# A recurrence and a highway layer on one core: loads of eight tokens per partition, and a new list of the order of work

## The chip, the cores and the metric

The kernel runs on one core of one Trainium2 chip. The metric is the device time of one execution, in microseconds (us); less is better. A profile is one such execution, recorded by the hardware profiler. Its span reaches from the first to the last recorded instruction; the execution's own time is a little longer.

## The reference, cut to what matters

```python
sig = 1.0 / (1.0 + np.exp(-f_logit))            # x, f_logit: (4, 6336, 256) fp32
f = lower_bound + (1.0 - lower_bound) * sig
i = 1.0 - f
for t in range(S):                              # S = 6336
    h = f[:, t] * h + i[:, t] * x[:, t]
    y[:, t] = h
x = y.reshape(25344, 256)
H = np.maximum(x @ w_h, 0.0)
T = 1.0 / (1.0 + np.exp(-(x @ w_t + b_t)))
out = T * H + (1.0 - T) * x
```

A linear recurrence runs along 6336 tokens for each of 4 batches and 256 channels. Two products with 256 x 256 weights follow for each token, and a gate that mixes the first with the recurrence's own output. 52.4 MB are read and 26.0 MB are written.

## The kernel before, in words

**Units, fronts and backs.** The tokens are cut into 24 units of 1024 neighbouring tokens of one batch, and one last unit with the 4 x 192 tokens that are left, on 96 partitions. The units go round the four batches, so that four recurrences run in turn. A unit lies in SBUF with tokens on 128 partitions and 8 tokens in each. Its recurrence is the "front", its layer the "back". The first three units and the last are cut further (`CUTS`): unit 0 into fronts of 2, 2 and 4 tokens per partition, units 1, 2 and the last into two fronts of 4. So there are 30 fronts: pieces 0 to 6 are small, pieces 7 to 27 are whole units (3 to 23), pieces 28 and 29 are the last unit's. There are 26 backs, 0 to 23 of a whole unit each.

**How the tokens lie** is set by `run(piece)` (L108 to L111). It says how many neighbouring tokens one partition holds in one run, so how long a contiguous stretch of memory a load brings to it: 4 tokens are 4 KB of fp32 in 256 channels. Where a whole unit of 8 has runs of 4, partition p holds tokens 4p to 4p+3 of the first 512 and the same of the second 512. Three places undo it, so that the recurrence sees the tokens in order:

- `load` (L102, its DMA on L106) brings `f_logit` (tile `lt`) and `x` (tile `xt`).
- `b_pe` (L209 to L217) transposes pairs of neighbouring tokens (two bf16 values seen as one fp32 word) on the tensor engine (PE) into PSUM tile `bT`, 128 columns at a time, and writes them at a stride of `run // 2` words: of two words where the run is 4.
- `decay_act` (L201 to L207) reads PSUM tile `uT`, which holds one token index after the other, with the tokens of a run innermost: at a step of 128 fp16 values.

**One front** takes these steps; the letters are those of the list that is told of below. L, X: loads. U: the gate `u`, a sigmoid on ScalarE (ACT, L154). P: the product `bv` of u and x for one pair of token indices, on GpSimd (POOL, L160); p is the same on VectorE (DVE, L166), taken for the two pieces in `EARLY`. A: transposes of u by PE (L198). F: the decay `f`, for each half of the channels, on ACT (L205). B: transposes of the pairs (L215). S: the scan along the tokens on DVE (L230), which gives tile `y`.

**One back** takes: Z, G: the two products with weights on PE (L245), tiles `zp` and `gp`; T: the sigmoid `t` on ACT (L251); D: `d`, on DVE (L256); E: `e`, d times t, on DVE (L166); H: the other part of e, on GpSimd (L160); O: matmuls that sum and transpose back (L296, L297); C: the copy of the result out of PSUM on ACT (L303), and V for a part of the last backs on DVE (L303); R: the store (L309). Of e, `shared(j)` columns are GpSimd's: 512 of 1024 in every whole back.

DVE's e and GpSimd's work share a port to SBUF, and the kernel has the next GpSimd product wait for a DVE product ahead of it in the list (`gpsimd_mul`, `port`).

**The order of the work** is a list written out, `PLAN`, of 1079 letters. Each letter issues the next instruction (or group) of its kind, and a digit behind A, B, Z, G and O names the PSUM slot. A and B share two slots, Z, G and O share three. Every engine runs its own in the order of the list, and SP's queue holds all loads and stores in that order; an instruction that waits holds back all behind it on its engine. SBUF tiles rotate: five each for `lt` and `xt`, two each for `bv`, `t`, `d` and `e`.

Of the kernel before, what the change touches and what calls it, by code (L numbers as in the profile page):

```python
# [19 lines left out]
def kernel(  # L20
# [19 lines left out]
    P = 128  # L40
    NH = D // P
    NB = 8
# [14 lines left out]
    units = [(P, NB, b, NB, s0) for s0 in range(0, S - rest, NB * P) for b in range(B)]  # L57
    units.append((rest // 2, NB, 0, 2, S - rest))
    fronts, backs = [], []
# [6 lines left out]

    LASTQ = 2

    EARLY = [(0, 0), (2, 0)]

# [29 lines left out]
    def load(i, name, src):  # L102
        u, j0, j1 = fronts[i]
        np_, j = units[u][0], run(fronts[i])
        t = fs[i][name] = new(name, [NB, D], FP32)
        pin(nc.sync.dma_start(t[:np_, :j1 - j0].rearrange("p (k j) d -> p k (j d)", j=j), tokens(src, u, j0, j1, j)))  # L106

    def run(piece):  # L108

        u, j0, j1 = piece  # L110
        return min(4, j1 - j0, units[u][3])  # L111

    def shape(piece):

        u, j0, j1 = piece
        return units[u][0], j1 - j0
# [34 lines left out]
    def gate(i):  # L151
        np_, nb = shape(fronts[i])
        u = fs[i]["u"] = new("u", [NB, D], FP16)
        pin(nc.scalar.activation(u[:np_, :nb], fs[i]["lt"][:np_, :nb], AF.Sigmoid, scale=-1.0))  # L154
# [13 lines left out]
    def product(i, k, mul):  # L168
        np_, _ = shape(fronts[i])
        if "bv" not in fs[i]:  # L170
            fs[i]["bv"] = new("bv", [NB // 2, D, 2], BF16)
        mul(inner(fs[i]["bv"][:np_, k:k + 1])[:, 0], fs[i]["u"][:np_, 2 * k:2 * k + 2],
            fs[i]["xt"][:np_, 2 * k:2 * k + 2])

    def width(piece):
        np_, nb = shape(piece)
        return np_ * nb
# [23 lines left out]
    def decay_act(i, h):  # L201

        np_, N, j = shape(fronts[i])[0], width(fronts[i]), run(fronts[i])
        f = fs[i]["f", h] = new("f", [NB * P], FP16)
        pin(nc.scalar.activation(f[:, :N].rearrange("p (k q j) -> p k q j", q=np_, j=j),  # L205
                                 fs[i]["uT", h].rearrange("p (k j q) -> p k q j", q=np_, j=j), AF.Identity,
                                 scale=ncc[:, h:h + 1], bias=1.0))  # L207

    def b_pe(i, m, slot):  # L209
        (np_, nb), r = shape(fronts[i]), run(fronts[i]) // 2  # L210
        for bT, h in filled(fronts[i], m, slot, fs[i], "bT", BF16):

            t = bT.bitcast(FP32).rearrange("p (k q j) -> p k j q", q=np_, j=r)
            for k in range(nb // 2):
                pin(nc.tensor.transpose(t[:, k // r, k % r],  # L215
                                        fs[i]["bv"][:np_, k, h * P:(h + 1) * P].rearrange("p d j -> p (d j)").bitcast(FP32),
                                        ident_f[:np_, :np_]))  # L217
# [41 lines left out]
    SHARE = 512  # L259

    def shared(j):

        return SHARE if width(backs[j]) == NB * P else 0

    def e_cols(j, a, e):
        if "e" not in bs[j]:
# [3 lines left out]
    def e_dve(j):  # L270
        vector_mul(*e_cols(j, 0, width(backs[j]) - shared(j)))

    def e_pool(j):
        gpsimd_mul(*e_cols(j, width(backs[j]) - shared(j), width(backs[j])))
# [37 lines left out]
    def each(pieces, count):  # L312
        return [(i, k) for i, piece in enumerate(pieces) for k in range(count(piece))]

    def halves_of(pieces):
        return each(pieces, lambda p: len(halves(p)))
# [11 lines left out]
        "U": (lambda i, _: gate(i), each(fronts, lambda p: 1)),  # L328
        "P": (lambda i, k: product(i, k, gpsimd_mul), [p for p in products if p not in EARLY]),
        "p": (lambda i, k: product(i, k, vector_mul), [p for p in products if p in EARLY]),  # L330
        "A": (decay_pe, halves_of(fronts)),
# [7 lines left out]
        "D": (d_dve, each(backs, lambda p: NH)),  # L339
        "E": (lambda j, _: e_dve(j), each(backs, lambda p: 1)),  # L340
        "H": (lambda j, _: e_pool(j), [(j, 0) for j in range(len(backs)) if shared(j)]),
        "O": (o_pe, groups),
        "C": (lambda j, q: o_copy(j, q, nc.scalar.copy, 0, group(j, q)[2]), [p for p in groups if group(*p)[2]]),
# [3 lines left out]
    }  # L347

    PLAN = (
        "LLXXLXQQUUA0pFFB1PSLXLXLXLSA0B1UFFpSSWWA0PFFUXLXLB1PSA0PSUFFUPPG0G1Z2B1DDSZ0STTA0B1PPHEFFUPSXXLA0SPF"  # L350
        "FUO1B0O2LLXXA1PSSPCCFFUPG0G1B0PPPDSSDZ2Z0A1A0TTFFEZ2B1Z0A0TTUFG1G2SDDB1HPPPPHPO0O1B0UCCSSZ2A1G0Z1B0E"
        "DTFTPPSPPPA1O2G0O1DHFUCCB1A0G0Z2Z1SFTTA1B0DEPSLLLXXRXRRLXRRRFUPG2O0B1O1A0DPPHCCG2FSDZ0Z1A1B0G2EPSTTF"
        "UPO0O1B1DPPHCCA0G2Z0SFDZ1A1B0EPSTFTUPG2O0A1B0O1DPPHCCG2Z0FSDA0B1Z1EPRRRRXLLSTFTPO2G0B0O1DPUCCESZ0G2A"
        "1Z1TFDB0A1G0PHPSDTFUO2B1O1CCPPPHSA0G0Z2Z1B1DFTEPSA0G0O2TPFDPPHB0O1G0A1UCCFSXLRXRRLRRRLLRXXDZ2Z1B0A1E"
        "PSTTFPO0G2B1A0O1DPPHCUCFSG0Z2Z1B1A0DEPSTTFPG0O2B0O1A1DPPHUCFCSG0Z2DA1B0Z1EPSG0PTFTDPPHB1O2O1G0A0UCCS"
        "Z2B1Z1FTDEPXRXRRRLRSTPA0O0G2O1B1DPPHFCCSA0G0Z2Z1B1DUFTEPSA0G0O2TPFCO1B0A1G2DPPHCSFUDZ0Z1A1B0G2EPSTTF"
        "PLLRRXLXRRXRRDPPHO0O1B0A1CCSFUG0Z2Z1A1B0DTTFEPSPG0O2O1B0A1DPPHCCFUSZ2G0A1B0Z1DEPSTTFPG0O2O1B0A1DPPHC"
        "CFUSG2Z0B1Z1A0RLRRRRXLRXXLLDEPSTFTPG2O0B0O1A1DPPHCUCFSG2Z0B0Z1A1DTTFEPSG2O0B0O1A1PDPPHCUCFSG2Z0B0Z1A"
        "1TFTDEPSPG2O0B1A0G1UCFDPPHSDO2Z0B1A0Z1TFTCPSPG0B0A1EZ1O2FTCUDSG0A1Z1B0RRRRRXRREDHFFO2G0B1TCPSRO1A0O2"
        "PCCFDSERG0G1RDSHZ2Z0B1DFTTSZ2G1O0HTTSDDCO2G1EERDO0CDO2CVRO1RCVZ0RCVTRTEO2O1CVRR"  # L360
    )
    assert all(PLAN.count(k) == len(places) for k, (_, places) in kinds.items())
    todo = {k: iter(places) for k, (_, places) in kinds.items()}
# [31 lines left out]
```

## Time and profile before

| | |
|---|---|
| time, median of 6 runs | 215.42 us (214.95 to 216.1) |
| the profiled execution: time, span | 215.08 us, 213.3 us |
| its granted tensor clock | 0.988 |
| busy: DVE, ACT | 196.0 us (92%), 194.6 us (91%) |
| busy: PE, weight loads | 188.9 us (89%), 132.5 us (62%) |
| busy: GpSimd | 164.9 us (77%) |
| moved by DMA | 78.68 MB, mean 369 GB/s, the load and store queue 92.4% of 16 engines |

Busy times are those of records. A record of ACT or DVE is longer than the step from one start to the next, because the next begins while the last results are still written: of two gates in the middle the record is 2.2 us and the step 1.8 us. Where "step" stands below, it is the distance between the starts of two instructions with no wait between them. The heading "idle before" in a group's row is the time for which the engine had no record, and what ended most of that time is named behind it.

### The profile page before, as it was taken

How to read it: one execution, taken by the hardware profiler on the slowest of the kernel's cores; microseconds unless marked ns; L12 is line 12 of the kernel's file. 1: busy time of each engine (PE TensorE's matmuls, PEld its weight loads, DVE VectorE, ACT ScalarE, POOL GpSimd, SP SyncE). 2: the span in 40 equal slices, each digit the busy share in tenths (PEclk: the TensorE clock that was granted, in tenths of full speed). 3: DMA queues.
4: the chain of work that ended last, by engine and by line, in shares of the span. 5: the costliest groups of instructions: out<-in, count | busy, mean ns of one | idle time of the engine just before them, and what ended most of it. 6: DMA issues, size and time to landing. Idle time of an engine off the chain costs nothing.

```text
span 213.3 us, 4602 instructions
## 1 busy us (share of the span) xinstructions
PE 188.9 (89%) x1800; PEld 132.5 (62%) x1800; DVE 196.0 (92%) x156; ACT 194.6 (91%) x194; POOL 164.9 (77%) x134
## 2 busy tenths in 40 slices
PE   0477798889999999999999999999999999999861
PEld 0244665666766665776575777577667667676651
DVE  1598698999999999999999999999999999999971
ACT  4559989999999999999999999999999999996851
POOL 4268987989789988978988897898898889646500
PEclk9999799999999999999999999999999999999998
DMA  3999999999999999999999999999999998547085
GB/s 98 403 418 422 423 416 420 422 416 416 423 416 422 416 417 420 417 420 416 422 420 417 419 416 421 420 407 419 417 409 366 369 286 330 174 184 288 7 349 195
DMA packets 22726, 78.68 MB, mean 369 GB/s; under 512 B 2353, under 2 KB 2865, under 8 KB 22705
## 3 DMA queue, kind: packets, MB, share of 16 engines
q1 hardware_dynamic: 22160, 78.39, 92.4%
q8 instruction: 14, 0.23, 0.4%
q10 hardware_dynamic: 544, 0.00, 0.1%
q14 instruction: 8, 0.06, 0.1%
HBM read 52.43 MB, written 25.95 MB: 368 GB/s over the span
## 4 chain that ended last, share of the span: by engine, by line
PE 46%; ACT 28%; DVE 14%; issue 5%; DMA 2%; POOL 2%; SPq 0%; ACTq 0%; DVEq 0%
PE gp L245 12%; ACT f L205 10%; PE zp L245 9%; ACT t L251 8%; DVE y L230 8%; PE op L296 7%; ACT u L154 7%; PE op L297 7%; PE bT L215 6%; PE uT L198 6%; DVE d L256 5%; ACT o L303 3%; DMA xt<-in_x_dram 2%; POOL e L160 1%; DVE e L166 1%
## 5 line engine op out<-in xcount | busy, mean ns | idle before, releaser
L160 POOL TENSOR_TENSOR bv<-u,xt 128x512 bf16<-128x512 f16 (+1 forms) x98 | 112.0, 1175 | 27.1 <-DVE e L166 8.5
L230 DVE TENSOR_TENSOR_SCAN y<-f,y,bT 128x1024 bf16<-128x1024 f16 (+3 forms) x56 | 106.8, 1920 | 0.7 <-ACT f L205 0.2
L205 ACT ACTIVATE f<-uT,ncc 128x1024 f16<-128x1024 f16 (+3 forms) x60 | 67.5, 1143 | 1.1 <-PE uT L198 1.1
L256 DVE SCALAR_TENSOR_TENSOR d<-y,ncc,gp 128x1024 bf16<-128x1024 bf16 (+1 forms) x52 | 62.6, 1211 | 1.2 <-PE gp L245 1.0
L251 ACT ACTIVATE t<-zp,bt 128x1024 bf16<-128x1024 f32 (+1 forms) x52 | 61.4, 1279 | 1.5 <-PE zp L245 1.0
L245 PEld LDWEIGHTS <-w_sb 128*128 128x128 f16 x400 | 37.9, 98 | 37.0 <-issue 5.7
L303 ACT COPY o<-op 128x1024 f32<-128x1024 f32 (+2 forms) x50 | 54.3, 1189 | 5.4 <-PE op L297 5.4
L154 ACT ACTIVATE u<-lt 128x2048 f16<-128x2048 f32 (+3 forms) x30 | 54.0, 1802 | 5.4 <-DMA lt<-in_f_logit_dram 5.2
L160 POOL TENSOR_TENSOR e<-d,t 128x1024 bf16<-128x1024 bf16 x24 | 51.6, 2151 | 8.7 <-DVE e L166 7.4
L297 PE MATMUL op<-ident_b,e 128*128 128x128 bf16 (+1 forms) x400 | 50.5, 222 | 2.8 <-DVE e L166 1.7
L245 PE MATMUL gp<-y,w_sb 128*128 128x512 bf16 (+1 forms) x200 | 51.4, 384 | 0.9 <-DVE d L256 0.8
L296 PE MATMUL op<-diag,y 128*128 128x128 f16 (+1 forms) x400 | 50.6, 221 | 0.8 <-ACT t L251 0.7
L245 PE MATMUL zp<-y,w_sb 128*128 128x512 bf16 (+1 forms) x200 | 49.5, 376 | 1.0 <-DVE y L230 0.8
L297 PEld LDWEIGHTS <-e 128*128 128x128 bf16 (+1 forms) x400 | 45.1, 115 | 7.0 <-DVE e L166 2.0
L296 PEld LDWEIGHTS <-y 128*128 128x128 bf16 (+1 forms) x400 | 45.2, 115 | 2.3
L215 PE MATMUL bT<-ident_f,bv 128*128 128x128 f32 (+1 forms) x200 | 32.3, 285 | 7.7 <-DVE y L230 2.1
L198 PE MATMUL uT<-ident_h,u 128*128 128x128 f16 (+1 forms) x400 | 31.7, 224 | 7.0 <-ACT u L154 5.5
L198 PEld LDWEIGHTS <-u 128*128 128x128 f16 (+1 forms) x400 | 26.9, 100 | 14.4 <-ACT u L154 5.8
L215 PEld LDWEIGHTS bT<-ident_f,bv 128*128 128x128 f32 (+1 forms) x200 | 23.0, 145 | 15.6 <-POOL bv L160 3.8
L166 DVE TENSOR_TENSOR e<-d,t 128x1024 bf16<-128x1024 bf16 (+1 forms) x26 | 18.4, 712 | 0.7 <-ACT t L251 0.5
L230 DVE TENSOR_TENSOR_SCAN y<-f,bT 128x512 bf16<-128x512 f16 (+2 forms) x8 | 10.5, 1343 | 3.2 <-PE bT L215 3.2
L303 DVE COPY o<-op 128x512 f32<-128x512 f32 (+1 forms) x4 | 2.8, 689 | 1.8 <-PE op L297 1.1
(20 smaller groups left out, 8.8 us busy)
## 6 DMA issues: line engine op xcount, KB each, us to landing
out_dram<-o SPq DMA_DIRECT2D x48, 512.0 KB, 13.6
lt<-in_f_logit_dram SPq DMA_DIRECT2D x21, 1024.0 KB, 14.9
xt<-in_x_dram SPq DMA_DIRECT2D x21, 1024.0 KB, 16.1
lt<-in_f_logit_dram SPq DMA_DIRECT2D x5, 512.0 KB, 7.8
xt<-in_x_dram SPq DMA_DIRECT2D x5, 512.0 KB, 8.6
xt<-in_x_dram SPq DMA_DIRECT2D x2, 384.0 KB, 10.2
lt<-in_f_logit_dram SPq DMA_DIRECT2D x2, 384.0 KB, 16.2
lt<-in_f_logit_dram SPq DMA_DIRECT2D x2, 256.0 KB, 4.1
```

Source lines behind the costliest of these rows:

```text
L154: pin(nc.scalar.activation(u[:np_, :nb], fs[i]["lt"][:np_, :nb], AF.Sigmoid, scale=-1.0))
L160: ins = pin(nc.gpsimd.tensor_mul(out_, a, b))
L198: pin(nc.tensor.transpose(uT[:, j * np_:(j + 1) * np_], fs[i]["u"][:np_, j, h * P:(h + 1) * P], ident_h[:np_, :np_]))
L205: pin(nc.scalar.activation(f[:, :N].rearrange("p (k q j) -> p k q j", q=np_, j=j), fs[i]["uT", h].rearrange("p (k j q) -> p k q j", q=np_, ...
L215: pin(nc.tensor.transpose(t[:, k // r, k % r], fs[i]["bv"][:np_, k, h * P:(h + 1) * P].rearrange("p d j -> p (d j)").bitcast(FP32), ident_ ...
L230: pin(nc.vector.tensor_tensor_scan(y, fs[i]["f", h][:, c:c + w], fs[i]["bT", h][:, c:c + w], 0.0 if prev is None else prev, op0=ALU.mult, ...
L245: pin(nc.tensor.matmul(p[:, a:e], w_sb[:, k, ki, h * P:(h + 1) * P], y_of(j)[:, ki, a:e], start=ki == 0, stop=ki == NH - 1))
L251: pin(nc.scalar.activation(bs[j]["t"][:, m, :width(backs[j])], bs[j]["zp", m], AF.Sigmoid, bias=bt[:, m:m + 1]))
L256: pin(nc.vector.scalar_tensor_tensor(bs[j]["d"][:, m, :width(backs[j])], y_of(j)[:, m], ncc[:, m:m + 1], bs[j]["gp", m], op0=ALU.mult, op1 ...
L296: pin(nc.tensor.matmul(o, y[:, h, cols], diag[:, h], start=True, stop=False))
L297: pin(nc.tensor.matmul(o, bs[j]["e"][:, h, cols], ident_b, start=False, stop=True))
L303: pin(copy(bs[j]["o", q][:np_, a:e], bs[j]["op", q][:np_, a:e]))
```

## The change

A run may hold eight tokens, so the 21 whole units that are one front (pieces 7 to 27) are loaded with 8 KB per partition in one stretch where there were two of 4 KB; the pairs of those pieces are written at a stride of four PSUM words instead of two, and their f is read with eight tokens innermost. Loads of pieces 0 to 6, 28 and 29, and all stores, keep their shapes. `EARLY` is empty: the first product of piece 0 and of piece 2 moves from DVE to GpSimd. The first three backs leave GpSimd no part of e: DVE makes all of it in one instruction of twice the size, and the list has three letters H fewer. The list is another one throughout; its first two and last two lines are shown.

```diff
-    EARLY = [(0, 0), (2, 0)]
+    EARLY = []
...
     def run(piece):
         u, j0, j1 = piece
-        return min(4, j1 - j0, units[u][3])
+        return min(8, j1 - j0, units[u][3])
...
     def shared(j):
-        return SHARE if width(backs[j]) == NB * P else 0
+        return SHARE if width(backs[j]) == NB * P and j >= 3 else 0
...
     PLAN = (
-        "LLXXLXQQUUA0pFFB1PSLXLXLXLSA0B1UFFpSSWWA0PFFUXLXLB1PSA0PSUFFUPPG0G1Z2B1DDSZ0STTA0B1PPHEFFUPSXXLA0SPF"
-        "FUO1B0O2LLXXA1PSSPCCFFUPG0G1B0PPPDSSDZ2Z0A1A0TTFFEZ2B1Z0A0TTUFG1G2SDDB1HPPPPHPO0O1B0UCCSSZ2A1G0Z1B0E"
...
-        "1TFTDEPSPG2O0B1A0G1UCFDPPHSDO2Z0B1A0Z1TFTCPSPG0B0A1EZ1O2FTCUDSG0A1Z1B0RRRRRXRREDHFFO2G0B1TCPSRO1A0O2"
-        "PCCFDSERG0G1RDSHZ2Z0B1DFTTSZ2G1O0HTTSDDCO2G1EERDO0CDO2CVRO1RCVZ0RCVTRTEO2O1CVRR"
+        "XLLLXXLXLQQUUA0A1PFFFUFUB0PSSB1A0FFPSSPB1A0XLLXLXXPFUFSSWWPB1A0G0Z1PFFUPSSDPXLLXLB0A1G2Z0PUTFFTPPB1S"
+        "SDUSSEZ1A0G0G2A1DDPFTFFPPZ1A0B1O0O2PSSTFECCUB0Z1B1G0G2SDSDA0Z0TUFTPPPPPPA0G1B1FXLLLXRRXLXDESA0Z0Z2O1"
...
+        "UCFPSO1PZ0CDTB1A0Z1G2SFTUHO0A0B1DFG1EPPPPSO2A0CCZ0DFB1O2Z1B0TCUTSESHPPG0A1Z2G1DDRRRRRRRRFFTA1B0O2Z0Z"
+        "1FCFSEHTTG2B1G0O1RSDDCO2SRHCZ0G1STRO2TDDEZ0CTERTG1O2O0DVDVCO2CREVO1CRO0RCVRR"
```

More of the change, by code (lines that the diff above doesn't have):

```diff
@@ L349 @@
     PLAN = (
-        "LLXXLXQQUUA0pFFB1PSLXLXLXLSA0B1UFFpSSWWA0PFFUXLXLB1PSA0PSUFFUPPG0G1Z2B1DDSZ0STTA0B1PPHEFFUPSXXLA0SPF"
-        "FUO1B0O2LLXXA1PSSPCCFFUPG0G1B0PPPDSSDZ2Z0A1A0TTFFEZ2B1Z0A0TTUFG1G2SDDB1HPPPPHPO0O1B0UCCSSZ2A1G0Z1B0E"
-        "DTFTPPSPPPA1O2G0O1DHFUCCB1A0G0Z2Z1SFTTA1B0DEPSLLLXXRXRRLXRRRFUPG2O0B1O1A0DPPHCCG2FSDZ0Z1A1B0G2EPSTTF"
-        "UPO0O1B1DPPHCCA0G2Z0SFDZ1A1B0EPSTFTUPG2O0A1B0O1DPPHCCG2Z0FSDA0B1Z1EPRRRRXLLSTFTPO2G0B0O1DPUCCESZ0G2A"
-        "1Z1TFDB0A1G0PHPSDTFUO2B1O1CCPPPHSA0G0Z2Z1B1DFTEPSA0G0O2TPFDPPHB0O1G0A1UCCFSXLRXRRLRRRLLRXXDZ2Z1B0A1E"
@@ L355 @@
[L355 to L358, printed above, removed]
-        "1TFTDEPSPG2O0B1A0G1UCFDPPHSDO2Z0B1A0Z1TFTCPSPG0B0A1EZ1O2FTCUDSG0A1Z1B0RRRRRXRREDHFFO2G0B1TCPSRO1A0O2"
@@ L360 @@
-        "PCCFDSERG0G1RDSHZ2Z0B1DFTTSZ2G1O0HTTSDDCO2G1EERDO0CDO2CVRO1RCVZ0RCVTRTEO2O1CVRR"
+        "XLLLXXLXLQQUUA0A1PFFFUFUB0PSSB1A0FFPSSPB1A0XLLXLXXPFUFSSWWPB1A0G0Z1PFFUPSSDPXLLXLB0A1G2Z0PUTFFTPPB1S"
+        "SDUSSEZ1A0G0G2A1DDPFTFFPPZ1A0B1O0O2PSSTFECCUB0Z1B1G0G2SDSDA0Z0TUFTPPPPPPA0G1B1FXLLLXRRXLXDESA0Z0Z2O1"
+        "UFTCTB0G0A1O1O2SDPPPFCCB1A0Z1G0O2FTUCB0G1PPPHPSDSEDPA1Z0Z2B0O1FTUCTESA1G0G1B0DDHPPPPSZ2O0O1FUTCCB1SA"
+        "0G2Z0B1FDUTPHPPSXXLRLRRRLRXLRRZ1A0G2O0PDTFCEEG1B1A0O2O0UFCCDSG1B0A1Z2Z0SDPHPPPPFTTA1B0O2O1G0HPSFCCZ2"
@@ new lines @@
+        "B1A0Z1DUTFTEG0O2PSPLXXRXRRRRDPPHCB1SA0O1G0Z2B1FCUTDEPSG1Z0A0O2FTCPDPPHB1A0Z1G0O2SFTCDEB0Z1A1G0PLLXRR"
+        "RRSDPPPUFTO2B0A1Z0G1SHDCFTEO2B0G0Z1A1PPPPCUFTSDHO2B0A1G0Z1SCFTO2B0A1DEPSZ1G0PPPCUFTDHO2B0A1O0G1SCFCD"
+        "EZ2B0A1Z0PSTFTPPPG1B1O2A0O0DUCFCSG1Z2A1B0HDELXLLRXRLLRXRRRRRXPSTFPPZ1G0O2B1DTCSZ1G2A0O0PHUFTCDEB1A0G"
+        "2Z1O0PSPFTCDPPHB0G1G2A1Z0UFTSA0B1FDEDSPO1O0Z2B0PPCCTPHSO1A1G0Z2B0UFTCDEPSA1G0Z2O1PPDB0FTCSA1Z2G0O1PH"
+        "FUCTDELXRRXXRRLRLXXRRRA1B0G0Z1PSFTO2DCB1A0G1Z0O2PPPHSUFCTDEB1A0Z1G2O0PSDFTCB0A1Z1G2SFPPPHDO0B1A0G2ET"
```

## The prediction

> **What bounds the kernel now.** I read the page's slices first (5.3 us each), then busy time by stretch, then ACT in the order of time at both ends.
>
> ```profile
> DVE  1598698999999999999999999999999999999971
> ACT  4559989999999999999999999999999999996851
> ...
> DMA  3999999999999999999999999999999998547085
> ```
>
> ```profile
> core 0: us, PE busy (x) PEld busy (x) DVE busy (x) ACT busy (x) POOL busy (x), PEclk, DMA share, GB/s
> 9.20:10.40 1.20, 0.58 (x2) 0.42 (x3) 0.88 (x2) 1.17 (x3) 0.00 (x0) 1.00 1.06 373
> 11.00:16.00 5.00, 3.79 (x21) 2.31 (x19) 4.74 (x6) 3.16 (x4) 3.12 (x3) 1.00 1.03 420
> 60.00:140.00 80.00, 77.23 (x769) 54.98 (x768) 79.53 (x55) 80.00 (x75) 70.12 (x53) 1.00 1.03 418
> ```
>
> Three things are full at once in the middle: DVE, ACT and the DMA engines. Which one sets the pace shows in the steps between starts. One unit costs ACT 1.80 (gate) + 2 x 1.00 (f) + 1.99 (two t) + 1.79 (two copies) = 7.58 us. DVE: 2 x 2.26 (scans) + 2 x 1.18 (d) + 0.58 (e) = 7.46. DMA: 3.15 MB at 418 GB/s = 7.53. PE: 16 product matmuls x 0.215, 32 of L296/L297 x 0.055, 16 transposes of u x 0.055, 8 of pairs x 0.109 = 6.95. The gates of pieces 11 and 26 start at 48.22 and 163.50: 7.69 us per unit. So ACT is the narrowest by a hair, and DMA's 7.53 lets loads run ahead: no gate waits for a load after 40 us. A faster DMA alone buys nothing there. What can be won lies at the ends, where ACT has gaps:
>
> ```profile
> 5.94 0.63 ACT L154 ACTIVATE u<-lt 128x512 f16<-128x512 f32 x1 [1.05 <-DMA lt<-in_f_logit_dram]
> ...
> 8.58 1.06 ACT L154 ACTIVATE u<-lt 128x1024 f16<-128x1024 f32 x1 [1.29 <-DMA lt<-in_f_logit_dram]
> ...
> 11.46 1.27 ACT L205 ACTIVATE f<-uT,ncc 128x512 f16<-128x512 f16 x2 [1.10 <-PE uT L198]
> ...
> 15.05 1.06 ACT L154 ACTIVATE u<-lt 128x1024 f16<-128x1024 f32 x1 [1.38 <-DMA lt<-in_f_logit_dram]
> ...
> 27.81 1.01 ACT L303 COPY o<-op 128x1024 f32<-128x1024 f32 x1 [0.89 <-PE op L297]
> ```
>
> ```profile
> 203.82 0.59 ACT L303 COPY o<-op 128x512 f32<-128x512 f32 x1 [1.14 <-PE op L297]
> ...
> 206.30 1.05 ACT L251 ACTIVATE t<-zp,bt 128x384 bf16<-128x384 f32 x2
> 208.63 0.58 ACT L303 COPY o<-op 96x512 f32<-96x512 f32 x1 [1.28 <-PE op L297]
> ```
>
> The brackets are ACT's idle time and who ended it. The first five (with two of 0.24 and 0.19) make 6.1 us; from 30.0 to 181 there is none. At the end ACT sits idle 1.14 us for a copy and only then does the last unit's t, on which e, the last matmuls and the last copies hang.
>
> **The parts, one by one.**
>
> *8 KB runs.* Between 9.2 and 10.4 us mostly the weights' 1 KB runs move, at 373 GB/s; 4 KB runs make 418 to 420. A fixed cost per run that explains both is 6 ns on each of 16 engines (43.9 ns per KB at 1 KB, 39.2 at 4 KB), and 8 KB would make 427 GB/s, my estimate from these rows: 2.46 us per 1 MB load for 2.51. The other end: 0. The 42 loads give 2.1 us of DMA time, nearly all hidden behind ACT's 7.58 us per unit; on the path lie the seven that come up to the load of lt of piece 10, 0.35 us. The Trainium skill speaks twice here: Perfetto Trace Analysis (DMA Optimizations) says that batching 2 KB into 4 or 8 KB can dramatically improve throughput, DMA: Bandwidth & Descriptors (Why small descriptors are slow) gives a few cycles per packet that matter at a few hundred bytes. The rows side with the second.
>
> *Pairs at a stride of four words.* The four transposes of one half, without waits: 0.60 us with a last record of 0.273, a step of 0.109 us for 128 columns, 0.85 ns a column, at a stride of two. The last unit's are at a stride of one: 0.083 us for 96, 0.86 ns. Contiguous is not faster, so I price four words at 0; it can't gain. The dear end is 0.213, this line's step at half clock (25.4 to 26.1 us): 8 x 0.104 = 0.83 us of PE per unit. PSUM — Partial Sum Buffer (Specifications, TRN2) has lines of 8 bytes and says that any non-contiguous pattern slows matmuls significantly, which speaks against this part; at a stride of two every word already has its own line, and the trace shows no cost. By that rule the sum would be that of the first rival.
>
> *f with eight tokens innermost.* Per added column, f costs 0.8 ns (0.41 us at 256 columns in runs of 2, 0.60 at 512 and 1.00 at 1024 in runs of 4), as the contiguous gate does (0.95 at 1024, 1.80 at 2048: 0.83). The step through PSUM stays 128 values. Price 0, since runs of 2 and of 4 lie on one line; dear end, the gate's rate, 0.03 ns x 1024 x 42 = 1.3 us; it can't gain, as 0.8 is there at either run.
>
> *No e on GpSimd for three backs, no product on DVE.* DVE: e of 2048 columns by the rows at 768 and 1024 (0.56 and 0.67) 1.1 us, 1.16 as two instructions, 0.58 before: +0.5 x 3; minus 2 x 0.62 for the products, of which the second is on the path. GpSimd: minus 3 x 2.13, plus 2 x 1.17. The matmuls that waited 1.11 us for GpSimd's e at 24.05 (and the copy behind them, 0.89) now wait for DVE. DVE's e holds GpSimd: the next product listed behind it waits. Behind e of back 0 that is P of piece 7, with 4 x 1.16 us up to its transposes: 27.4 to 32.1, needed at 33.2, so covered with 1 us left.
>
> *The new list, start.* Every load is as far back as the bytes ahead of it. The walk uses the trace's landings by place in the queue (4.24, 5.91, 6.73 us; then 0.63 per 256 KB). x now comes first, so the first gate starts at 5.94, not 4.26: 1.7 us later. Then, on ACT: gate, gate at 6.75, three f to 8.5, gate 2 to 9.45, f to 9.86, idle to 11.15 for lt of piece 3, gate 3 to 12.1, f of piece 2 to 13.3, idle 0.7 for transposes that wait for their PSUM slot, f 14.6, gate 4 to 15.55, f 16.15, idle 0.7, f of piece 4 to 18.05, gates 5 and 6 to 19.95, t, two f, t to 23.15, gate 7 to 24.95. Before, the same set ended at 25.89. Next f, t, f, f, t, f without a gap to 30.15 (DVE's second scan pair starts at 8.6 and its e of back 0 ends at 27.4, PE's O of back 0 after d of back 1, at 29.6), two copies to 31.95, gate 8 to 34.05 behind its load (32.25: one x load more is ahead of it than before, when it landed at 29.93). Before, this set ended at 35.82. Gates 9 and 10 end at 36.85 and 41.65; before, with one f moved to the same side, 43.43. **Gain at the start 1.8 us.** DVE is 2.4 ahead at that point (44.6 against 47.07 with the same set done), so it is not late next; the loads are, gate 10's by 0.3 us.
>
> *The new list, middle.* The same work per unit, in another order: price 0, ends -0.1 (what the old one loses: 7.69 - 7.58) and +0.25 per unit, half the 0.5 us that ACT waits at 200.74 for a copy. SP's queue has loads and stores mixed anew; the shortest leads of a load in the trace are 1.4 to 1.7 us (x of pieces 19 and 27, lt of 16).
>
> *The new list, end.* The last unit's Z and both t now stand ahead of the last whole back's copies: their 1.0 us fills ACT's idle 1.14 (and what copies 22 leave). DVE then has e right behind its own work. From the old last d's end (204.1), less the start's 1.8 (202.3): two of the copies' halves (0.6 each) now come ahead of e, and wait some 0.6 for ACT's halves, to 204.1, e to 204.6, two groups of O to 205.6, last copy 206.3, store 2.4 us to 208.7, where 212.2 was: 3.5 in all, **1.7 of it here**.
>
> **Sum.** The walks make 3.5 us. They charge nothing for hand-overs; ACT alone has idles of 0.16 to 0.68 us five times between 190 and 201 in the old list, which such a walk would miss. I keep three quarters: 2.6 us. Profiled execution: span 213.3 - 2.6 = 210.7, plus the 1.8 outside it, 212.5 for 215.08; the median of the six runs is 0.34 above that execution, so **212.8 us**.
>
> **Rivals.**
> 1. *The stride costs; slower.* Place: PE's transposes of pairs in pieces 7 to 27. PE has 7.58 - 6.95 = 0.63 us to spare per unit, so it decides from a step of 0.19. At 0.213 PE needs 7.78: +0.2 over 7.58 for 21 units, 4.2, and the waits of DVE's scans that PE with no slack brings, by 0.1 each unit 2.1. Less the gain of 2.6: 219. For it speaks only that the trace has no stride of four; against it, 0.85 and 0.86 ns.
> 2. *The new middle stalls; slower.* f, t and copies alternate singly where they ran in pairs, so every ACT instruction has another engine's hand-over ahead of it. At +0.25 per unit over 19 units: +4.7 - 2.6, 217.5. It decides from 0.14. Against it: PE has slack, and each engine's sum is unchanged.
> 3. *What is won at the start is lost to the loads or at the end.* Loads land 0.3 us ahead of gates 9 and 10, with no lead behind them; a hold of 1 us on each of two eats the start's gain, and the tail's order may hold at V, which waits for the ACT copy of the same group. 215.4.
> 4. *Runs of 8 KB are moved as 4 KB.* The start loses its 0.35: within the forecast's own range, 213.1.
>
> **Chances.** Forecast and rival 4, 211.3 to 214.7: 0.6. Rival 3, 214.8 to 216.0: 0.15. Rival 2: 0.15, half of it below 217.3. Rival 1: 0.1. The range 211.3 to 217.3 leaves out some 0.2. About 0.3% (0.65 us) is what this measurement can tell from no change: faster 0.6, within 0.15, slower 0.25.
>
> **What would show it.** Steps of L215 at 0.109 for 128 columns (rival 1: above). f at a step of 1.00. Gate 7 at 23 us and gate 8 near 32, with ACT's gap ahead of the copies at 27 us gone. The middle's GB/s up by some per cent while loads run ahead, or unchanged because ACT holds the buffers; 7.6 to 7.7 us between gates (rival 2: 7.9). No t among ACT's last four rows. I am wrong if gates late in the middle wait for loads, or if DVE's e of backs 0 to 2 takes over 1.6 us beside GpSimd's products.

## The result, and the profile after

| | before | after |
|---|---|---|
| time, median | 215.21 us (70 runs, 214.53 to 216.29) | 214.28 us (35 runs, 213.29 to 215.16) |
| ratio, 95% interval | | 0.9949 (0.994 to 0.9958) |
| the profiled execution: time, span | 215.08, 213.3 us | 214.35, 212.6 us |
| load and store queue, share of 16 engines | 92.4% | 90.4% |
| packets | 22726 | 17350 |

The kernel became 0.5% faster: 1.1 us by the ratio (0.9 by the medians) where 2.6 were forecast. First the page's slices of after (5.3 us each).

```profile
DVE  1269999999999999999999999999999999999980
ACT  2757999999999999999999999999999999997760
...
DMA  5999999999999999999999999999999996242465
```

DVE is now full from the fourth slice on and ACT from the fifth; before, it was the eighth and the seventh: the holes around 27 us are gone. But DVE's second and third slices are emptier (2 and 6 for 5 and 9). The same windows as before (the columns are those that the prediction shows):

```profile
9.20:10.40 1.20, 0.39 (x2) 0.00 (x0) 0.70 (x2) 1.20 (x3) 0.95 (x1) 1.00 1.02 416
11.00:16.00 5.00, 3.31 (x22) 2.49 (x20) 3.22 (x4) 3.05 (x5) 4.30 (x4) 1.00 1.04 410
60.00:140.00 80.00, 77.72 (x768) 54.79 (x766) 79.40 (x54) 80.00 (x75) 71.34 (x56) 1.00 1.02 423
```

The middle moves 423 GB/s for 418, within the estimate of 427, and ACT stays at 80.00 of 80: no stall, and no gain there either. From 11 to 16 us DVE works 3.22 us of 5 (4.74 before) and ACT 3.05 (3.16 before). ACT's rows there, in order of time:

```profile
5.91 0.63 ACT L154 ACTIVATE u<-lt 128x512 f16<-128x512 f32 x1 [3.11 <-DMA lt<-in_f_logit_dram]
7.47 0.63 ACT L154 ACTIVATE u<-lt 128x512 f16<-128x512 f32 x1 [0.93 <-DMA lt<-in_f_logit_dram]
...
11.85 1.06 ACT L154 ACTIVATE u<-lt 128x1024 f16<-128x1024 f32 x1 [1.27 <-DMA lt<-in_f_logit_dram]
...
15.17 0.69 ACT L205 ACTIVATE f<-uT,ncc 128x512 f16<-128x512 f16 x1 [1.10 <-PE uT L198]
...
18.73 1.27 ACT L205 ACTIVATE f<-uT,ncc 128x512 f16<-128x512 f16 x2 [1.36 <-PE uT L198]
...
24.93 1.93 ACT L154 ACTIVATE u<-lt 128x2048 f16<-128x2048 f32 x1
...
33.66 2.00 ACT L154 ACTIVATE u<-lt 128x2048 f16<-128x2048 f32 x1
```

Against the walk: gate 1 starts at 7.47 (6.75), gate 3 at 11.85 (11.15), f of piece 4 at 18.73 after 1.36 us of idle (0.7), gate 7 at 24.93 (23.15), gate 8 at 33.66 (32.25). So ACT ends gate 7's set 0.84 us later than before, where the walk had it 0.94 earlier. DVE in the same stretch:

```profile
14.16 2.45 DVE L230 TENSOR_TENSOR_SCAN y<-f,y,bT 128x512 bf16<-128x512 f16 x2 [1.32 <-PE bT L215]
16.53 2.30 DVE L148 SCALAR_TENSOR_TENSOR w_sb<-o,cc 128x512 f16<-128x512 f32 x2
18.75 2.32 DVE L230 TENSOR_TENSOR_SCAN y<-f,bT 128x512 bf16<-128x512 f16 x2
20.99 1.25 DVE L256 SCALAR_TENSOR_TENSOR d<-y,ncc,gp 128x1024 bf16<-128x1024 bf16 x1
22.16 2.44 DVE L230 TENSOR_TENSOR_SCAN y<-f,y,bT 128x512 bf16<-128x512 f16 x2
```

From 14.16 us (piece 2's scans) to its last d at 203.6 DVE's idle time sums to 0.9 us, none of it over 0.11 at once before 76 us (before: 4.5 us, from 13.31): DVE starts late and then hardly rests. The two W take 2.30 us together (1.39 before), because a product of GpSimd runs beside the second, from 17.09 on:

```profile
17.09 2.76 POOL L160 TENSOR_TENSOR bv<-u,xt 128x512 bf16<-128x512 f16 x2 [1.58 <-DMA xt<-in_x_dram]
```

The end, on ACT:

```profile
201.90 1.05 ACT L251 ACTIVATE t<-zp,bt 128x384 bf16<-128x384 f32 x2 [0.33 <-DVE e L166]
203.70 0.59 ACT L303 COPY o<-op 128x512 f32<-128x512 f32 x1 [0.75 <-DVE o L303]
204.82 0.59 ACT L303 COPY o<-op 128x512 f32<-128x512 f32 x1 [0.54 <-DVE o L303]
206.15 1.07 ACT L303 COPY o<-op 96x512 f32<-96x512 f32 x2 [0.74 <-DVE o L303]
```

As forecast no t is among ACT's last four instructions (all copies), and the last copy ends at 207.2 (209.8 before, there on DVE): 2.6 us won. But the last store, issued at 207.7, lands at 211.04, where before's landed at 212.20. The stores of either kernel's last 2 us, before first:

```profile
L309 SPq DMA_DIRECT2D out_dram<-o x2: 324/336/347, 209.2 to 209.8; - x2
...
DMA to landing us min/median/max: 2.4/2.4/2.4
```

```profile
L309 SPq DMA_DIRECT2D out_dram<-o x3: 333/377/572, 206.8 to 207.7; - x3
...
DMA to landing us min/median/max: 3.3/3.3/3.3
```

Of the 2.6 us won at the copy 1.2 arrive at the last landing, and 0.7 at the end of the span (1.53 us lie between them, 1.07 before).

### The profile page after: what moved, and what is told of

Same layout as the page of the kernel before. It is cut to its first block, busy times and chain, and to the rows that moved or that the text cites. A ratio compares the mean times of both kernels' runs of the same rounds, so it can differ in the third digit from the quotient of the medians.

```text
span 212.6 us, 4616 instructions
## 1 busy us (share of the span) xinstructions
PE 187.8 (88%) x1800; PEld 131.4 (62%) x1800; DVE 195.3 (92%) x154; ACT 193.7 (91%) x194; POOL 160.9 (76%) x133
## 2 busy tenths in 40 slices
DMA packets 17350, 78.69 MB, mean 370 GB/s; under 512 B 2352, under 2 KB 2864, under 8 KB 11952
## 3 DMA queue, kind: packets, MB, share of 16 engines
q1 hardware_dynamic: 16784, 78.39, 90.4%
## 4 chain that ended last, share of the span: by engine, by line
ACT 35%; PE 31%; issue 13%; DVE 13%; DMA 3%; SPq 1%; POOL 1%; ACTq 1%; DVEq 0%; POOLq 0%
ACT t L251 11%; PE zp L245 9%; ACT o L303 8%; ACT u L154 8%; ACT f L205 8%; PE gp L245 6%; DVE y L230 6%; DVE d L256 5%; PE bT L215 4%; PE uT L198 4%; PE op L296 3%; PE op L297 3%; DMA xt<-in_x_dram 3%; DVE e L166 1%; SPq L106 1%
## 5 line engine op out<-in xcount | busy, mean ns | idle before, releaser
L160 POOL TENSOR_TENSOR bv<-u,xt 128x512 bf16<-128x512 f16 (+1 forms) x100 | 114.6, 1181 | 31.6 <-DVE e L166 14.1
L205 ACT ACTIVATE f<-uT,ncc 128x1024 f16<-128x1024 f16 (+3 forms) x60 | 64.9, 1094 | 2.5 <-PE uT L198 2.5
L251 ACT ACTIVATE t<-zp,bt 128x1024 bf16<-128x1024 f32 (+1 forms) x52 | 62.8, 1226 | 0.4 <-DVE e L166 0.3
L154 ACT ACTIVATE u<-lt 128x2048 f16<-128x2048 f32 (+3 forms) x30 | 52.6, 1758 | 5.3 <-DMA lt<-in_f_logit_dram 5.3
L245 PE MATMUL zp<-y,w_sb 128*128 128x512 bf16 (+1 forms) x200 | 50.5, 377 | 0.9 <-DVE d L256 0.6
L296 PE MATMUL op<-diag,y 128*128 128x128 f16 (+1 forms) x400 | 49.2, 219 | 1.8 <-DVE d L256 0.7
L160 POOL TENSOR_TENSOR e<-d,t 128x1024 bf16<-128x1024 bf16 x21 | 44.8, 2135 | 7.3 <-DVE e L166 2.6
L297 PE MATMUL op<-ident_b,e 128*128 128x128 bf16 (+1 forms) x400 | 49.3, 219 | 0.0
L198 PE MATMUL uT<-ident_h,u 128*128 128x128 f16 (+1 forms) x400 | 32.1, 225 | 10.0 <-ACT u L154 7.5
L166 DVE TENSOR_TENSOR e<-d,t 128x1024 bf16<-128x1024 bf16 (+2 forms) x26 | 19.0, 736 | 0.1
L230 DVE TENSOR_TENSOR_SCAN y<-f,bT 128x512 bf16<-128x512 f16 (+2 forms) x8 | 10.4, 1336 | 4.1 <-PE bT L215 4.1
(19 smaller groups left out, 10.9 us busy)
```

The costliest lines, as they stand in the source:

```text
L160: ins = pin(nc.gpsimd.tensor_mul(out_, a, b))
L198: pin(nc.tensor.transpose(uT[:, j * np_:(j + 1) * np_], fs[i]["u"][:np_, j, h * P:(h + 1) * P], ident_h[:np_, :np_]))
L230: pin(nc.vector.tensor_tensor_scan(y, fs[i]["f", h][:, c:c + w], fs[i]["bT", h][:, c:c + w], 0.0 if prev is None else prev, op0=ALU.mult, ...
L245: pin(nc.tensor.matmul(p[:, a:e], w_sb[:, k, ki, h * P:(h + 1) * P], y_of(j)[:, ki, a:e], start=ki == 0, stop=ki == NH - 1))
L251: pin(nc.scalar.activation(bs[j]["t"][:, m, :width(backs[j])], bs[j]["zp", m], AF.Sigmoid, bias=bt[:, m:m + 1]))
L296: pin(nc.tensor.matmul(o, y[:, h, cols], diag[:, h], start=True, stop=False))
```

## The experiments

"ratio" is the time against the kernel before, with its 95% interval. Own times are those of profiled executions.

### The parts of the change, each alone

**Runs of eight in the old list.**

```diff
-        return min(4, j1 - j0, units[u][3])
+        return min(8, j1 - j0, units[u][3])
```

> The kernel before with runs of eight tokens and nothing else changed (its own list, its own e and products). My theory: ACT and DVE set the pace from 40 us on and hold the buffers, so faster loads buy only the start: the DMA rate in the middle rises from 418 to 422-424 GB/s, the pair transposes stay at a step of 0.109 us, and the time is 0 to 0.4 us below before (ratio 0.998 to 1.000). Rival: the whole gain of the change (1 us) is that of the runs; then this kernel stands at a ratio of 0.995.

215.20 us, ratio 0.9983 (0.9962 to 1.0004). Nothing that can be told from no change: the middle of the interval is a gain of 0.4 us, its end 0.8, and a cost of the stride of four words doesn't show.

**Runs of four in the new list** (the same line, the other way).

> The changed kernel with runs of at most four tokens again (new list, no e on GpSimd for three backs, no products on DVE). My theory: the list and not the runs made the gain, so 213.8 to 214.7 us, a ratio of 0.994 to 0.998. Rival: the runs made it; then a ratio of 1.000, or above if the list costs.

214.52 us, ratio 0.9955 (0.9938 to 0.9972). The gain is there without the runs; 0.24 us of median is what they add, not to be told from nothing.

**No e on GpSimd, no product on DVE, in the old list:** `EARLY = []`, `and j >= 3` in `shared`, the first three H left out, p written as P.

> The kernel before, its list kept, but GpSimd makes no part of e for the first three backs and all products of the first pieces (three letters H dropped, two p made P). My theory: DVE gains 1.2 us of products and pays some 1.6 us for e, and PE waits for the whole e instead of GpSimd's half; within 0.5 us of before (ratio 0.998 to 1.002). Rival: DVE's longer e is what held the start of the changed kernel: 1 us or more above before (1.005).

215.32 us, ratio 0.9988 (0.9963 to 1.0012). No difference.

### The end

**The old list with the new order at its end.** The first try took the new letters from the last unit's T on:

```diff
-...DFTTSZ2G1O0HTTSDDCO2G1EERDO0CDO2CVRO1RCVZ0RCVTRTEO2O1CVRR
+...DFTTSZ2G1O0HCSTRO2TDDEZ0CTERTG1O2O0DVDVCO2CREVO1CRO0RCVRR
```

> The kernel before, with the new list's order for the last instructions only, from the last unit's first t on. My theory: the last copy ends 1.5 to 2 us earlier, but the stores behind it find the DMA engines still busy with those issued just ahead, so the last store lands only 0.5 to 1.0 us earlier: ratio 0.995 to 0.998. Rival, the prediction's own: a store takes 2.4 us from its issue whatever is ahead of it, and all of 1.7 us is won: ratio 0.992.

218.57 us, ratio 1.0135 (1.0096 to 1.0174): a miss. Z of back 24 stayed in PSUM slot 2, as in the old list, and the new order's next O asks for that slot, so it waits until t has read it. ACT's rows:

```profile
200.45 1.01 ACT L303 COPY o<-op 128x1024 f32<-128x1024 f32 x1 [1.72 <-PE op L297]
...
204.01 1.01 ACT L303 COPY o<-op 128x1024 f32<-128x1024 f32 x1 [1.59 <-PE op L297]
```

Two waits of 1.7 and 1.6 us come from one digit. It says nothing of the order. The second try takes the slots along, from Z of back 24 on:

```diff
+...DFTTSO2HCZ0G1STRO2TDDEZ0CTERTG1O2O0DVDVCO2CREVO1CRO0RCVRR
```

> The kernel before, with the new list's order and PSUM slots for the last 41 instructions, from the two Z and G of the last unit's first back on, so that no slot of the old order is left to wait for. My theory: the last copy ends 1.5 to 2.5 us earlier than before (209.8), but the last three stores then stand behind 1.5 MB of other stores, and the end comes only 0.5 to 1.2 us earlier: ratio 0.994 to 0.998. Rival: a store always takes 2.4 us; ratio 0.990 to 0.992. Rival: the end of the list gained nothing and all of the 1 us is from elsewhere: 1.000.

214.97 us, ratio 0.9983 (0.9966 to 1.0). The last copy ends at 208.5 (209.8), the last store goes from 209.03 to 212.37, 3.3 us, where before's took 2.4: what the copies win, the store gives back. The start of this execution was slower: its last scan ends at 201.47 us (200.99). Counted from there, the last copy comes 1.7 us earlier than before (7.06 for 8.77), the last landing 0.3 (10.91 for 11.20).

**Which bytes make the last store long?** After with three quarters of back 23's stores left out:

```diff
+        np_ = units[u][0] // (4 if j == 23 else 1)
```

> The changed kernel, but of the last whole back's two stores only the first quarter of the partitions is stored (0.79 MB of output left out). My theory: at the end the DMA engines are the bound (the last copy ends at 207.2 and stores land until 211.0), so 0.79 MB at 420 GB/s less makes the last store land 2.4 to 2.8 us after its issue, 0.6 to 1.0 us earlier: ratio to before 0.990 to 0.992. Rival: the 3.3 us from issue to landing are the store's own; then no change from the changed kernel, ratio 0.995.

214.29 us, ratio 0.9941 (0.9917 to 0.9964), the same as after; the last store still takes 3.1 us. My theory named the wrong bytes. So the last unit's own, with five sixths of back 24's store left out:

```diff
+        np_ = 16 if j == 24 else units[u][0]
```

> The changed kernel, but the store of the last unit's first back goes out for 16 of its 96 partitions (0.33 MB of output left out). My theory: the last three stores, 0.79 MB in runs of 2 KB issued within 1 us, are what keeps the last one 3.3 us on its way instead of 2.4; with the first of them nearly gone the last lands 2.4 to 2.7 us after its issue: 0.6 to 0.9 us less than the changed kernel, ratio to before 0.991. Rival: 3.3 us whatever is ahead: 0.995.

213.22 us, ratio 0.9919 (0.9892 to 0.9947). The three last stores:

```profile
L310 SPq DMA_DIRECT2D out_dram<-o x3: 332/347/380, 207.5 to 208.4; - x3
...
DMA to landing us min/median/max: 2.0/2.2/2.5
```

The last takes 2.5 us where it took 3.3, and lands 10.0 us behind the end of the last scan instead of 10.9. So the bytes of back 24's store make this 0.9 us: in after the last unit's three stores (0.79 MB) are issued within 1 us and land 0.5 us behind one another; in the same last stretch before had two.

**Copies that don't share a group.** In backs 23 and 24, ACT's half of each group waits for DVE's (0.75, 0.54 and 0.74 us above). Here each group is copied whole, by one engine (the letters of the copies that this saves leave the list):

```diff
-        return q * size, g, g // 2 if size == QB else (g if q % 2 == 0 else 0)
+        return q * size, g, g if q % 2 == 0 else 0
```

> The changed kernel, but each of the last backs' groups is copied by one engine whole (even groups ACT, odd ones DVE) where ACT and DVE each took half of it; in the changed kernel's trace the two halves run one after the other (202.97, 203.70, 204.10, 204.82). My theory: the two groups of back 23 are copied side by side, their stores start up to 1 us earlier and the DMA engines, which hold the end, finish 0.5 to 1.0 us earlier: ratio to before 0.990 to 0.993. Rival: the last copy (205.4 to 207.2) holds the end, and it isn't touched: ratio 0.995.

214.19 us, ratio 0.9939 (0.9916 to 0.9963): not to be told from after. With the last e ahead of DVE's copy as well:

```diff
-...O2O0DVDVCO2CREVO1CRO0RCVRR
+...O2O0DDECVRO1O2RCRO0CVRR
```

> The changed kernel with whole copies (each group by one engine, as in the run with whole copies) and the last e put ahead of the copies of back 23 on DVE, the last matmuls behind it spread over the free slots. My theory: the last copy ends 0.6 to 1.0 us earlier than 207.2; the three stores of the last unit stand closer together, so about half of it reaches the end: ratio to before 0.990 to 0.993. Rival: stores hold the end whatever the copies do: 0.994, as with whole copies alone.

214.67 us, ratio 0.998 (0.9963 to 0.9997), worse. The chain up to the copies did not get shorter: behind the end of the last scan the last copy ends 7.1 us later, as in after, and the last landing comes 11.0 us later (10.9). The last three stores, issued from 206.8 to 208.1, take 3.6 to 3.9 us each. So this run doesn't tell what a shorter chain would buy.

### The start

Four suspects: PE's half clock, W beside GpSimd, the order of the first loads, and when those land.

**The tensor clock.** 18 matmuls of zeros, 10 from 1.9 us on and 2 behind each of four early transposes:

```diff
+    def busy_pe(n):
+        t = psum("2", [NB * P], "dummy", FP32)
+        for _ in range(n):
+            pin(nc.tensor.matmul(t[:, :512], ident_b, zeros, start=True, stop=True))
```

> The changed kernel with 18 matmuls more, of zeros into a PSUM slot that nobody reads: ten from about 2 us on, while PE has nothing to do, and two behind each of four early groups. My theory: the walk of the start failed because PE had half clock until 20.3 us (17.0 before), so that ACT waited 1.10 and 1.36 us for transposes; with full clock by 8 us both waits shrink by half and the start gains 0.5 to 1.5 us: ratio to before 0.988 to 0.993. Rival: the loads' landings hold the start and the clock costs nothing: ratio 0.995, the same as the changed kernel.

213.75 us, ratio 0.992 (0.9902 to 0.9937), faster than after (0.994 to 0.9958). The clock is full from 6.8 us, half from 10.2 to 17.0, and full again (after: full from 20.3). But in this run W took 1.47 us for 2.38 too, since GpSimd's product came later, so it isn't the clock alone.

**W without GpSimd beside it.**

```diff
-...PFUFSSWWPB1A0...
+...PFUFPSSWWB1A0...
...
+        port.append(pin(nc.vector.scalar_tensor_tensor(w_sb...
```

(one P is listed ahead of the scans, and the next waits for both W)

> The changed kernel with the second product of piece 3 ahead of the first scans of piece 2 in the list, and GpSimd's next product made to wait for the two weight instructions on DVE (L148). In the changed kernel the second of them takes 1.65 us beside a GpSimd product, where alone it takes 0.74. My theory: DVE has no gap from 14.2 us to the end, so 0.9 us less on it there ends up in the time: ratio to before 0.990 to 0.993. Rival: the loads and ACT hold the start and the middle; DVE waits elsewhere for what it gains: 0.995, the same as the changed kernel.

214.19 us, ratio 0.9967 (0.9948 to 0.9985): no difference to after in the median. W is short, as intended:

```profile
13.74 2.45 DVE L230 TENSOR_TENSOR_SCAN y<-f,y,bT 128x512 bf16<-128x512 f16 x2 [1.33 <-PE bT L215]
16.11 1.39 DVE L148 SCALAR_TENSOR_TENSOR w_sb<-o,cc 128x512 f16<-128x512 f32 x2
17.54 2.33 DVE L230 TENSOR_TENSOR_SCAN y<-f,bT 128x512 bf16<-128x512 f16 x2
```

**The first loads as lt, lt, x** (`XLLLXX` becomes `LLXLXX`).

> The changed kernel with the first loads in the order lt, lt, x instead of x, lt, lt. The first gate then starts at 4.3 us instead of 5.9. My theory: the gates of pieces 2 to 4 still wait for loads that land when they landed, so the early gate is paid back by 15 us: ratio to before 0.994 to 0.996. Rival: the late first gate is what the start lost: 1 us or more is won, 0.990.

214.15 us, ratio 0.9951 (0.9933 to 0.9968). The first gate starts at 4.4 us; nothing of it is left.

**Do they add?** Clock and W; those and the loads; those and whole copies.

> The kernel after with the 18 dummy matmuls of e7 (they warm the tensor clock) and with the edit of e9 (GpSimd's next product waits for both W, one product listed ahead). Theory (the start is held by the loads up to gate 8 and by PE's slow transposes of pairs in turn; W beside GpSimd is a loss only where DVE has no time, and with the clock warm DVE is ahead): nothing to be won beyond e7, 0.990 to 0.993. Rival (the clock hid what W costs, so that the two add): W's 0.9 us comes off too, 0.988 or less.

> e13 with the first loads as lt, lt, x (e10's edit). Theory (the bytes ahead of gate 8 are the same, and gate 8 starts at 33.3 to 33.7 in every list that has the new middle): the first gate starts at 4.4 and nothing of it is left at gate 8; same as e13 within 0.002. Rival (with the clock warm and W short, the early gate is kept): 0.985 to 0.988.

> e14 with the copies of the last whole backs' groups made whole by one engine each (e8's edit), so every edit that did no harm in one. Theory (the end is held by the last unit's three stores, which queue at the DMA engines; copies that end 0.2 us earlier only make the queue longer): 0.988 to 0.993, not to be told from e13. Rival (the edits add): 0.986 or less.

213.62 us, 0.9924 (0.9895 to 0.9952); 212.94, 0.9891 (0.9865 to 0.9916); 212.75, 0.9887 (0.986 to 0.9914). Clock and W don't add. With lt first the six times (212.65 to 213.22) lie all below those without it (213.34 to 213.99), which my theory excluded. What differs shows when the landings of the loads are put beside the times. DVE's work without rest begins with piece 2's scans. Their bracket in after names the transposes bT, and the rows lead from these back to x of piece 1, the fifth load:

```profile
9.45 3.57 POOL L160 TENSOR_TENSOR bv<-u,xt 128x512 bf16<-128x512 f16 x3 [1.67 <-DMA xt<-in_x_dram]
10.68 0.67 PE L215 MATMUL bT<-ident_f,bv 128*128 128x128 f32 x2 [1.09 <-POOL bv L160]
11.45 1.38 DVE L230 TENSOR_TENSOR_SCAN y<-f,y,bT 128x256 bf16<-128x256 f16 x2 [0.49 <-PE bT L215]
12.98 1.09 PE L215 MATMUL bT<-ident_f,bv 128*128 128x128 f32 x4 [0.77 <-DVE y L230]
```

GpSimd's product waits for this x, piece 1's transposes for the product, piece 1's scans for the transposes, and piece 2's transposes for these scans, whose PSUM slot they take (B1 in the list both times).

| | 5th load lands | 7th load lands | scans start | both W, sum of records | clock full from | own time | own time less 7th landing |
|---|---|---|---|---|---|---|---|
| after | 9.31 | 11.83 | 14.16 | 2.38 | 20.3 | 214.35 | 202.5 |
| runs of four | 9.69 | 12.21 | 14.54 | 2.37 | 21.4 | 214.91 | 202.7 |
| whole copies | 9.03 | 11.56 | 13.88 | 2.38 | 21.1 | 213.98 | 202.4 |
| whole copies, e first | 9.23 | 11.75 | 14.09 | 2.38 | 21.9 | 215.01 | 203.3 |
| lt first | 8.94 | 11.45 | 13.79 | 2.38 | 19.8 | 213.74 | 202.3 |
| less of back 23's store | 8.75 | 11.29 | 13.60 | 2.38 | 22.3 | 214.51 | 203.2 |
| less of back 24's store | 9.32 | 11.84 | 14.18 | 2.38 | 22.2 | 214.26 | 202.4 |
| W apart | 8.89 | 11.42 | 13.74 | 1.48 | 19.3 | 213.47 | 202.1 |
| clock | 9.41 | 11.93 | 14.27 | 1.47 | 6.8 | 213.95 | 202.0 |
| clock, W | 9.19 | 11.71 | 14.04 | 1.46 | 6.5 | 213.73 | 202.0 |
| clock, W, lt first | 8.58 | 11.05 | 13.32 | 1.47 | 6.9 | 213.01 | 202.0 |
| the same, whole copies | 8.68 | 11.22 | 13.12 | 1.47 | 4.7 | 212.80 | 201.6 |

(In the last four rows the clock fell back to half once more, from 10.2, 9.9, 10.4 and 8.1 us to 17.0, 16.7, 13.8 and 11.5.)

The seventh load is lt of piece 3; gate 3 waits for it, and the f of piece 2 stand behind gate 3 on ACT. It lands 2.5 us behind the fifth in every row, so both keep time with the scans: they start 4.85 us behind the fifth (4.74 and 4.44 in the last two rows) and 2.3 behind the seventh (1.9 in the last). But it is not the f that the scans wait for. In after the first f of piece 2 is done at 13.49, 0.67 us ahead of the scans; in the last row the scans start 0.33 us before the second f is done (13.45). In every row they start 0.1 us behind the last transpose of piece 2 (where the second f ends later than it by 0.02 to 0.06 us, the bracket names f). What the clock does to this chain shows in the last row too: full from 11.5 us on, the four transposes take 0.67 us for 1.09, and the scans start 4.4 us behind the fifth load. In the two rows above "clock, W, lt first" the clock had lapsed to half by then, and the 4.85 stand.

The seventh load lands anywhere between 11.0 and 12.2 us, and the execution's time goes with it. By these single executions a stretched W is worth some 0.4 us (202.3 to 202.7 against 202.0), half of what it measures, and from the scans to the end of the piece 8 scan that starts at 44.01 in after DVE takes 32.1 us there and 31.4 to 31.7 in three executions with W short. The median of twelve with W apart doesn't show it, so what it is worth in the time stays open. The 203.2 and 203.3 are executions in which the clock came at 22.3 and 21.9 and DVE stood idle 0.83 us at 21.7 and 0.41 at 22.2. So lt first won here because its loads landed early; why they did wasn't tried further. The order itself may have a part: with lt, lt, x in front (the old list's order too) the third load landed at 6.7 to 7.1 us in seven of eight profiled executions and at 7.5 in the other, with x, lt, lt at 6.9 to 7.8 in nine.

**Why the loads land late.** Two small loads on ACT's queue, lb and bt, are moved element by element (544 packets, nearly all of 4 bytes). This one issues bt behind the weights, on SP:

```diff
-    nc.scalar.dma_start(bt, moe_b_t.rearrange("(h p) -> p h", p=P))
...
+        if k == 1:
+            pin(nc.sync.dma_start(bt, moe_b_t.rearrange("(h p) -> p h", p=P)))
```

> The kernel after with one small load moved: the bias bt (272 packets, nearly all of 4 bytes) is issued behind the weights on SP's queue and not at 1.28 us on ACT's. In seven profiled runs with the new list unchanged up to there, DVE's third pair of scans (piece 1's second, S2) starts 6.71 to 6.73 us behind the landing of the third load, which lands at 6.9 to 7.8 us; DVE has no gap behind it and the last d starts 189.4 later. Theory (the 4-byte packets of bt, which move at 4.5 to 6.5 us while only 0.33 MB of loads come in 1.5 us, set that landing): third load at 6.4 to 6.9, S2 at 13.1 to 13.6, ratio to before 0.991 to 0.993. Rival (the queue is slow at the beginning whatever lies beside it): third load at 6.9 to 7.8 as in the other runs, ratio 0.9935 to 0.9965.

(The "third pair" of its text is piece 2's, as above.) 213.45 us, ratio 0.9917 (0.9893 to 0.9941; after's, 0.994 to 0.9958, just touches it). The DMA view from 4.5 to 6.0 us, after first:

```profile
DMA packets 440, 0.34 MB, mean 225 GB/s; under 512 B 278, under 2 KB 278, under 8 KB 440
## 3 DMA queue, kind: packets, MB, share of 16 engines
q1 hardware_dynamic: 180, 0.34, 64.1%
q10 hardware_dynamic: 260, 0.00, 9.3%
```

```profile
DMA packets 238, 0.54 MB, mean 358 GB/s; under 512 B 31, under 2 KB 31, under 8 KB 238
```

Without the 260 small packets (q10), 1.5 us bring 0.54 MB and not 0.34, though these packets themselves take only 9.3% of the engines' time. The third load lands at 6.09 (7.45 in after), the fifth at 8.53 (9.31), the seventh at 11.07, and the scans start at 13.38, 4.85 us behind the fifth as in the table. This profiled execution, 214.38 us, is the slowest of its six (the others 212.93 to 213.82): its clock came at 21.6 us, and DVE waited 0.56 us just then, own time less landing 203.3 as in the two such rows above.

**All of them together**, the fastest version:

> e15 (warm clock, W apart from GpSimd's products, lt first, whole copies) with bt behind the weights as well: the version with every edit. In e15 the third load landed at 6.83, S2 started at 13.12. Theory of the 4-byte packets: third load at 6.2 to 6.4, 0.4 to 0.6 less, 0.9855 to 0.987. Rival (what is early at the beginning is held by the transposes or by the loads of the later pieces, or e15's landing has nothing left to win): 0.988 to 0.990.

212.51 us, ratio 0.9867 (0.9844 to 0.989). The seventh load lands at 10.57, the scans start at 12.41:

```profile
12.41 2.45 DVE L233 TENSOR_TENSOR_SCAN y<-f,y,bT 128x512 bf16<-128x512 f16 x2 [1.09 <-PE bT L218]
14.78 1.39 DVE L151 SCALAR_TENSOR_TENSOR w_sb<-o,cc 128x512 f16<-128x512 f32 x2
16.08 2.33 DVE L233 TENSOR_TENSOR_SCAN y<-f,bT 128x512 bf16<-128x512 f16 x2
```

Here too the scans start 0.1 us behind piece 2's last transpose (it ends at 12.32) and ahead of the end of the second f (12.81).

With the late landing, the stretched W and the half clock mended (full from 6.8 us on in this execution), DVE's scans start even ahead of the walk (13.4 there, worked out below), and the time comes to the forecast's 212.8; the whole copies may have a part in it; the parts weren't told apart.

## Why the prediction was half right

**The new list, start: the step that failed.** Walked 1.8, measured 0.8. "DVE is 2.4 ahead at that point (44.6 against 47.07), so it is not late next": at the same point DVE was at 46.3, 0.8 us ahead. Between piece 2's scans and this point lie, in after, 31.2 us of DVE's work without the stretch of W, so the walk's 44.6 means scans at 13.4. Of the 1.65 us that are missing, their start at 14.16 makes 0.75, and W beside GpSimd's product 0.9, a wait that the walk never priced. The first of these comes from the sentence ahead of it: the walk took "the trace's landings by place in the queue (4.24, 5.91, 6.73 us)" as fixed; the third was 7.45, and all behind it came 0.7 later (x of piece 1 at 9.31 for 8.6, lt of piece 3 at 11.83 for 11.15). Over the profiled executions of the new list with its own loads the third was 6.9 to 7.8. One trace, of the other order, gave one draw of a number that scatters by 0.9 us, and the small packets beside it are a cause (the run with bt moved; that the rest of the scatter has the same cause isn't shown). And the walk followed ACT; DVE's chain has one line in it, "DVE's second scan pair starts at 8.6". By the walk's own landings x of piece 1 is there at 8.6, and GpSimd's product of 1.16 us and the transposes come between; the first two pairs started at 9.70 and 11.45. ACT shows the same loss: walked 1.8 ahead where gate 8's set is done and gate 10's, it was 0.35 and 0.1 ahead. Its waits for transposes were longer than walked (1.10 and 1.36 us for 0.7 each), and the clock has a part in that: eight transposes of u at the walk's 0.055 us are 0.44, their records at half clock took 1.0 to 1.1 us, and 0.6 at full clock.

**The new list, end: right up to the copies, wrong for the store.** Behind the end of the last scan (200.15 us for 200.99) the last copy ends 7.07 us later, for 8.77: the 1.7 of the walk. But the last landing comes 10.90 us later, for 11.20, so 0.3 of it arrive there. "Store 2.4 us" was before's price, for stores that went out apart. Three together took 3.3 (shown by leaving out most of one). 0.46 us more is lost between the last landing and the end of the span: 1.53 us for 1.07, in the kernels with the whole new list; with the new end alone it is 1.07. What that is stays open. With it the span ends 12.42 us behind the last scan, for 12.28: in these two executions nothing of the new end is left, and the 0.7 us are the start's.

**8 KB runs.** In the range, 0 to 0.4 us; 423 GB/s in the middle while ACT holds the pace, as forecast. A packet of 8 KB took 309 ns, one of 4 KB 159 (medians), so one run fewer saves 9 ns where 6 were estimated.

**Stride of four words.** Right: the transposes of pairs keep their record of 273 ns and their step of 0.109 us. The rows of before (strides of one and two) carried over; the rule of PSUM — Partial Sum Buffer (Specifications) in the Trainium skill, that non-contiguous patterns slow matmuls, shows in no run here at this stride. Rival 1 is out.

**f with eight innermost.** Right: 1.00 us.

**e on DVE alone.** Right: steps of 1.11 to 1.15 us for 1.1, and taking it from GpSimd in the old list changed nothing.

**Rivals.** 2 (the middle) is out: between 55 and 180 us what ACT's steps exceed the median of their form by sums to 0.7 us, 0.9 before. 3 named half of what happened (the start lost) and the wrong wait: gates 5 to 10 had their loads 1.4 us ahead or more, the loss lay in the first loads, on the way to DVE. Keeping three quarters of the walk was too much: of its 3.5 us, 2.6 reached the last copy, 1.2 the last landing and 0.7 the end of the span.

## What to carry to other kernels

A walk through a start must be made on every engine that will be full behind it, from the one instruction after which it hardly rests, back through every engine that this one waits for; here the whole time followed the start of that one scan. Two things that keep the same distance in every trace need not be cause and effect: only a run that parts them tells. A landing read from one trace is one draw: look at what shares the queue with the first loads, element-wise loads of constants above all, and move them behind. At the end the price of a store depends on what goes out in the microsecond beside it.

## What the runs showed of the hardware

**The clock follows the products, not the transposes.** In the 14 profiled executions without dummy matmuls, full clock was first granted 1.2 to 4.3 us behind the first product matmul and never ahead of it, wherever that lay (14.6 to 15.7 us with the old list, 17.7 to 18.9 with the new). Transposes alone didn't bring it in any of them; that it was the gaps between them that held the clock back isn't ruled out by these. In the run with clock and W, six dummies stand among the transposes here:

```profile
10.20:16.80 6.60, 6.13 (x29) 3.78 (x30) 4.40 (x6) 3.37 (x6) 4.84 (x5) 0.50 1.04 413
```

PE is busy 6.13 of 6.60 us at a clock of 0.50; full clock came back at 16.7 us, behind the dummies and ahead of the first product (18.4). TensorE: Matmul & The Clock Gate (Part 4: PE-mode transpose) of the Trainium skill says that transposes don't count as busy for the gate in the same way; these rows agree. By moving the first product from 14.6 to 18.5 us the new list kept the early transposes at half clock.

**Two engines, one PSUM group.** Where ACT and DVE copy halves of the same group, they go one after the other. In after DVE goes first (202.97 and 204.10) and ACT's rows wait for it (203.70 and 204.82); before, ACT goes first and DVE waits:

```profile
204.44 0.69 DVE L303 COPY o<-op 128x512 f32<-128x512 f32 x1 [0.29 <-ACT o L303]
```

Whether the chip or the program's order makes them wait isn't shown.

**DVE's W against GpSimd.** The second W took 1.66 us for 0.74 beside a product, and the next product 1.62 for 1.17: both lose.
